# Two gamma loads issued by GpSimd, and the value products of the first two pairs taken in halves of the contraction

## The chip, the cores and the metric

The kernel runs on one core of a Trainium2 chip. The metric is device time in microseconds (us) of one execution; each kernel is executed several times, in rounds with the kernel before on the same chip. Every execution reports two numbers: the time, and the span, which is what the profile covers, from its first to its last instruction. Faster and slower are given at 2%.

PE is the matmul engine, DVE is VectorE, ACT is ScalarE, POOL is GpSimd, SP is SyncE; "SPq" is an instruction of SP's queue that issues a transfer. A turn is a transpose by PE, a cast turns a landed float32 tile into bfloat16. Batch 0's 512 main tokens are worked in two halves of 256; the second is the "second token half". A pair is two times 128 of the 1536 feed-forward columns (blocks 0 and 1 of the weights are the first two pairs), a step is 128 of the 512 rows over which a product sums. The state is the product `kv`.

## The reference, cut to what matters

```python
kv  = einsum('bhsd,bhse->bhde', k, v)                  # batch 8, heads 8, seq 576, head_dim 64
out = einsum('bhsd,bhde->bhse', q, kv)
out = out / sqrt(mean(out*out, -1) + 1e-6) * g_norm
x   = out.transpose(0, 2, 1, 3).reshape(4608, 512)
xn  = x / sqrt(mean(x*x, -1) + 1e-6) * moe_rms_g
g   = xn @ w_gate                                      # 512 x 1536
y   = (g * sigmoid(g) * (xn @ w_val)) @ w_out          # 1536 x 512
```

Both gammas (`g_norm`, `moe_rms_g`) are small vectors. The kernel folds them into the rows of the gate and value weights: those come in as float32, are multiplied by `rowscale` and rounded to bfloat16 once ("rounding" below).

## The kernel before

The order of instructions on each engine is the program's. The program is a long start (batch 0, weights, batch 1, up to about 55 us) and then seven like stages in which PE works without a gap. Only the start is touched. Cuts are marked with `...`.

```python
# loads, in this order; load_kv brings one slice j of k or v
for j in (0, 1):
    load_kv(0, "k", nc.sync, slice(j, j + 1))
    load_kv(0, "v", nc.scalar, slice(j, j + 1))
SC.preload_act_table(ACT.Sqrt)
nc.scalar.dma_start(out=gam[0:NS, :], in_=moe_rms_g...)      # gamma, 2 KB
nc.scalar.dma_start(out=gam[NS : NS + 1, :]..., in_=g_norm...)
load_q0(0, nc.sync)                                          # batch 0's query, first half
for j in (2, 3):
    load_kv(0, "k", nc.sync, slice(j, j + 1))
    load_kv(0, "v", nc.sync, slice(j, j + 1))
load_q0(1, nc.sync)
load_w("g", (0, 1), False)
load_w("v", (0, 1), True)        # value weights of the first two pairs: steps 0,1 then steps 2,3
...
# GpSimd rounds value weights (block, contraction step); ScalarE does step 3
for blk, s in ((0, 0), (0, 1), (1, 0), (0, 2), (1, 1), (1, 2)):
    round_w(blk, "v", s, GP)
...
xs = [Z.scale(c, oZ[c]) for c in range(2)]                   # rows of the second token half
for u in range(2):
    ffn.half_unit(first[1], u, wv_sb, u, 0, 256)             # value products, first pair
for u in range(2):
    x_turn(Z, u, xs[u], DVE)                                 # turns of the second token half
for u in range(2):
    ffn.half_unit(second[1], u, wv_sb, 2 + u, 0, 256)        # value products, second pair
...
load_kv(1, "v", nc.sync)
load_wo(0, (2,))                                             # output weights, block 0, second half
load_q(1)                                                    # batch 1's query
load_wo(1)
...
for c in range(4):
    down_part(c, 0, 2)
att1.kv_products()
...                                                          # casts of batch 1's query
att1.kv_copy()                                               # state out of PSUM: ScalarE and DVE
...
down_part(0, 2, 4)
turns.q_turn(0, SC)                                          # PE turns batch 1's query
down_part(1, 2, 4)
turns.q_turn(1, DVE)
for c in range(2, 4):
    down_part(c, 2, 4)
```

Of the kernel before, what the change touches and what calls it, by code (L numbers as in the profile page):

```python
# [20 lines left out]
def kernel(  # L21
# [12 lines left out]
    nc = tc.nc  # L34
# [10 lines left out]
    NS = d_model // 128  # L45
# [30 lines left out]
    PE, DVE, SC, GP = nc.tensor, nc.vector, nc.scalar, nc.gpsimd  # L76
# [3 lines left out]
    gam = consts.tile([8, 128], FP32, name="gam")  # L80
# [11 lines left out]
    wv_sb = consts.tile([128, NS, d_ff], BF16, name="wv_sb")  # L92
# [91 lines left out]
    def round_w(blk, name, s, engine):  # L184
        j0, j1 = W_BLOCKS[blk]
        dst = {"g": wg_sb, "v": wv_sb}[name][:, s, j0 * 128 : j1 * 128]
        src = w_st[name, blk][:, s, :]
        if engine is SC:
            SC.activation(out=dst, in_=src, func=ACT.Copy, scale=rowscale[:, s : s + 1])
        else:  # L190
            engine.tensor_scalar(  # L191
                out=dst, in0=src, scalar1=rowscale[:, s : s + 1], scalar2=1.0, op0=OP.mult, op1=OP.mult
            )
# [49 lines left out]
    xnts = {}  # L243
# [15 lines left out]
    def to_rows(x, n, c, ps, engine):  # L259

        for j in range(NS):
            PE.matmul(
                ps[:, j, :], lhsT=x[:, 2 * j : 2 * j + 2, :], rhs=identity, is_transpose=True,
                start=(j == 0), stop=(j == NS - 1),
            )
        cast(engine, xnts[n][:, :, 128 * c : 128 * c + 128], ps)
# [198 lines left out]
    class Ffn:  # L465
# [25 lines left out]
        def half_unit(self, ps, u, wt, j, lo, hi):  # L491

            for s in range(NS):
# [2 lines left out]
                    rhs=xnts[self.n][:, s, lo:hi], start=(s == 0), stop=(s == NS - 1),  # L496
                )

        def up_pair(self, i, lo, banks=None):

            banks = banks or self.pair_banks()
            for k, wt in enumerate((wg_sb, wv_sb)):
                for u in range(2):
                    self.half_unit(banks[k], u, wt, 2 * i + u, lo, lo + 256)
            return banks
# [81 lines left out]
    for j in (0, 1):  # L587
        load_kv(0, "k", nc.sync, slice(j, j + 1))
        load_kv(0, "v", nc.scalar, slice(j, j + 1))
    SC.preload_act_table(ACT.Sqrt)  # L590
    nc.scalar.dma_start(out=gam[0:NS, :], in_=moe_rms_g.rearrange("(s p) -> s p", p=128))
    nc.scalar.dma_start(
        out=gam[NS : NS + 1, :].rearrange("o (i d) -> o i d", i=2),
        in_=g_norm.rearrange("(o d) -> o d", o=1).unsqueeze(1).to_broadcast([1, 2, D]),
    )
# [33 lines left out]
    Z = Cols(0, 256, 512, qt0, sqt0, "Z")  # L629
# [44 lines left out]
    def x_turn(cols, c, x, engine, p=att_pool, name="att_ps"):  # L674
        bank = p.tile([128, MAIN], FP32, name=name)
        to_rows(x, cols.n, cols.lo // 128 + c, bank.bitcast(BF16)[:, 0:512].rearrange("p (j t) -> p j t", j=NS), engine)
# [15 lines left out]
    for j in (0, 1):  # L692
# [29 lines left out]
        out=gsq, in0=gcol, scalar=1.0 / d_model, in1=gcol, op0=OP.mult, op1=OP.mult  # L722
# [24 lines left out]
    xs = [A.scale(c, oA[c]) for c in range(2)]  # L747
# [4 lines left out]
        x_turn(A, i, xs[i], DVE, *((ops_pool, "o_ps") if i else ()))  # L752
    round_w(1, "g", 2, DVE)
    round_w(1, "g", 3, SC)
    for blk, s in ((0, 0), (0, 1), (1, 0), (0, 2), (1, 1), (1, 2)):
        round_w(blk, "v", s, GP)
    ffn = Ffn(0)
    first, second = ffn.pair_banks(), ffn.pair_banks()
# [12 lines left out]
        round_w(blk, "v", 3, SC)  # L771
    SC.preload_act_table(ACT.Silu)
    xs = [Z.scale(c, oZ[c]) for c in range(2)]
    for u in range(2):
        ffn.half_unit(first[1], u, wv_sb, u, 0, 256)
    for u in range(2):
        x_turn(Z, u, xs[u], DVE)
    for u in range(2):
        ffn.half_unit(second[1], u, wv_sb, 2 + u, 0, 256)
    ffn.gate_pair(0, 0, first)  # L780
    ffn.gate_pair(1, 0, second)
    for name in ("g", "v"):
# [149 lines left out]
    xs = [F.scale(c, F.outa[c]) for c in range(4)]  # L932
# [50 lines left out]
    for n in range(1, B + 1):  # L983
        ffn = Ffn(n)
# [11 lines left out]
        if n < B:  # L996
# [5 lines left out]
            for i in range(2):  # L1002
                u = o0 + 2 * i
# [63 lines left out]
```

## Time and profile before

| | before |
|---|---|
| time, first three runs | 319.34, 320.76, 320.80 us |
| median of six runs | 320.06 us |
| span of the profiled run | 317.5 us |
| PE busy | 309.2 us, 97% |
| second token half starts (PE) | 21.71 us |
| batch 1's query is cast | 41.74 us |
| first query turn of batch 1 (PE) | 42.63 us, after 0.46 us of idle |

How to read it: PE at 97% says only that PE is rarely idle. What may shorten the time is found by asking, at each idle stretch of PE in the start, which thing came last. The lines for that are in the prediction.

### The profile page before, as it was taken

How to read it: one execution, taken by the hardware profiler on the slowest of the kernel's cores; microseconds unless marked ns; L12 is line 12 of the kernel's file. 1: busy time of each engine (PE TensorE's matmuls, PEld its weight loads, DVE VectorE, ACT ScalarE, POOL GpSimd, SP SyncE). 2: the span in 40 equal slices, each digit the busy share in tenths (PEclk: the TensorE clock that was granted, in tenths of full speed). 3: DMA queues.
4: the chain of work that ended last, by engine and by line, in shares of the span. 5: the costliest groups of instructions: out<-in, count | busy, mean ns of one | idle time of the engine just before them, and what ended most of it. 6: DMA issues, size and time to landing. Idle time of an engine off the chain costs nothing.

```text
span 317.5 us, 6031 instructions
## 1 busy us (share of the span) xinstructions
PE 309.2 (97%) x2371; PEld 149.9 (47%) x2371; DVE 180.5 (57%) x378; ACT 175.7 (55%) x323; POOL 21.4 (7%) x46
## 2 busy tenths in 40 slices
PE   7899999999999999999999999999999999999995
PEld 3585455444444444444444444444444444444443
DVE  3676658579339913892289327941795079504310
ACT  3577457485667465746683768376745374233321
POOL 1274350100000000000000000000000000000000
PEclk9999999999999999999999999999999999999999
DMA  7999999695369167904790489939003610230014
GB/s 277 351 387 387 376 374 343 146 280 196 94 178 369 59 145 194 359 5 113 191 375 19 100 170 231 330 68 200 2 0 61 139 66 3 59 140 3 0 33 100
DMA packets 60712, 54.95 MB, mean 173 GB/s; under 512 B 36232, under 2 KB 45708, under 8 KB 60684
## 3 DMA queue, kind: packets, MB, share of 16 engines
q1 hardware_dynamic: 60304, 53.92, 57.2%
q10 hardware_dynamic: 380, 0.66, 0.6%
q8 instruction: 18, 0.29, 0.4%
q14 instruction: 10, 0.08, 0.1%
HBM read 37.75 MB, written 9.44 MB: 149 GB/s over the span
## 4 chain that ended last, share of the span: by engine, by line
PE 84%; DMA 10%; SPq 3%; ACT 1%; POOL 1%; issue 0%; DVE 0%
PE g_ps L477 27%; PE o_ps L519 26%; PE v_ps L477 26%; DMA st<-in_q_dram 6%; DMA st<-in_moe_w_gate_dram 3%; PE att_ps L286 1%; SPq L199 1%; PE v_ps L519 1%; DMA out_dram<-o_sb 1%; PE att_ps L326 1%; POOL wg_sb L191 1%; SPq L182 1%; SPq L119 1%; PE o_ps L326 0%; PE g_ps L519 0%
## 5 line engine op out<-in xcount | busy, mean ns | idle before, releaser
L483 DVE TENSOR_TENSOR h_sb<-silu,v_ps 128x512 bf16<-128x512 bf16 x104 | 71.1, 684 | 100.4 <-ACT silu L482 68.0
L477 PE MATMUL g_ps<-xnt,wg_sb 128*128 128x512 bf16 x416 | 106.9, 379 | 0.0
L477 PE MATMUL v_ps<-xnt,wv_sb 128*128 128x512 bf16 x416 | 106.8, 379 | 0.0
L482 ACT ACTIVATE silu<-g_ps 128x512 bf16<-128x512 f32 x104 | 62.1, 597 | 70.2 <-PE g_ps L477 58.1
L519 PE MATMUL o_ps<-wo_sb,h_sb 128*128 128x512 bf16 x396 | 87.8, 379 | 0.0
L477 PEld LDWEIGHTS <-wv_sb 128*128 128x128 bf16 x416 | 40.7, 98 | 49.1
L519 PEld LDWEIGHTS <-h_sb 128*128 128x128 bf16 x420 | 40.6, 98 | 47.7 <-issue 0.4
L477 PEld LDWEIGHTS <-wg_sb 128*128 128x128 bf16 x416 | 39.6, 98 | 46.4
L104 ACT COPY o_sb<-o_ps 128x512 f32<-128x512 f32 (+1 forms) x34 | 19.7, 581 | 40.5 <-PE o_ps L519 39.7
L373 DVE TENSOR_TENSOR xna<-outa,s1y 128x512 bf16<-128x512 bf16 x28 | 17.9, 684 | 0.0
L104 ACT CAST vb<-st 128x576 bf16<-128x576 f32 x25 | 15.7, 673 | 3.7 <-DMA st<-in_v_dram 3.7
L356 DVE TENSOR_REDUCE ssq<-sqt 128x16 f32<-128x1024 bf16 x14 | 17.1, 1220 | 0.5
L356 DVE TENSOR_REDUCE ssq<-sq 128x16 f32<-128x1024 bf16 x14 | 17.1, 1220 | 0.5
L104 ACT CAST qb<-st 128x512 bf16<-128x512 f32 (+1 forms) x30 | 16.2, 602 | 2.1 <-DMA st<-in_q_dram 2.0
L104 ACT CAST kb<-st 128x576 bf16<-128x576 f32 x20 | 12.5, 673 | 0.0
L341 ACT ACTIVATE sq<-att_ps 128x512 bf16<-128x512 f32 x14 | 7.6, 594 | 4.3 <-PE att_ps L326 3.6
L355 DVE TENSOR_TENSOR sq<-sq,gsq 128x512 bf16<-128x512 bf16 x14 | 5.9, 422 | 4.9 <-ACT sq L341 4.9
L619 PE MATMUL att_ps<-kv_all 128*128 128x512 bf16 (+1 forms) x23 | 7.5, 445 | 1.2 <-DVE sel L608 1.2
L106 DVE CAST kb<-st 128x576 bf16<-128x576 f32 x12 | 5.7, 498 | 3.8 <-DMA st<-in_k_dram 3.8
L106 POOL CAST wo_sb<-st 128x512 bf16<-128x512 f32 x12 | 7.2, 632 | 7.4 <-DMA st<-in_moe_w_out_dram 7.4
L341 ACT ACTIVATE sqt<-o_ps 128x512 bf16<-128x512 f32 x14 | 7.6, 597 | 0.0
L347 ACT CAST outa<-o_ps 128x512 bf16<-128x512 f32 x14 | 7.5, 591 | 0.0
(145 smaller groups left out, 179.6 us busy)
## 6 DMA issues: line engine op xcount, KB each, us to landing
st<-in_k_dram SPq DMA_DIRECT2D x7, 1152.0 KB, 10.2
st<-in_v_dram SPq DMA_DIRECT2D x7, 1152.0 KB, 12.3
out_dram<-o_sb SPq DMA_DIRECT2D x14, 512.0 KB, 3.1
st<-in_q_dram SPq DMA_DIRECT2D x6, 1024.0 KB, 7.8
st<-in_moe_w_out_dram SPq DMA_DIRECT2D x6, 512.0 KB, 10.4
st<-in_moe_w_gate_dram SPq DMA_DIRECT2D x4, 512.0 KB, 10.1
st<-in_moe_w_val_dram SPq DMA_DIRECT2D x4, 512.0 KB, 9.4
st<-in_k_dram SPq DMA_DIRECT2D x4, 288.0 KB, 4.1
```

The source lines that it names most:

```text
L104: engine.copy(out=dst, in_=src)
L106: engine.tensor_copy(out=dst, in_=src)
L341: SC.activation(out=self.in_place(self.sq[i][:, 0], g), in_=bank, func=ACT.Square)
L347: SC.copy(out=self.in_place(rows, g), in_=bank)
L355: DVE.tensor_tensor(out=sq[:, 1], in0=sq[:, 0], in1=gsq8, op=OP.mult)
L356: DVE.reduce_sum(out=self.ssq[:, c], in_=sq, axis=AX.X)
L373: DVE.tensor_tensor(out=self.xna[c], in0=self.outa[c], in1=self.alpha[:, c, :].to_broadcast([128, H, D]), op=OP.mult)
L477: PE.matmul(ps, lhsT=wt[:, s, j * 128 : (j + 1) * 128], rhs=x[:, s, :], start=(s == 0), stop=(s == NS - 1),)
L482: SC.activation(out=silu, in_=g_ps, func=ACT.Silu)
L483: DVE.tensor_tensor(out=self.h[:, j, :], in0=silu, in1=v_ps, op=OP.mult)
L519: PE.matmul(self.o_ps[c], lhsT=self.h[:, j, c * 128 : (c + 1) * 128], rhs=wo_sb[:, j, :], start=(j == 0), stop=(j == NF - 1),)
L619: PE.matmul(ps[:, 0:w], lhsT=warm_sb[:, 0:128], rhs=warm_sb[:, 0:w], start=True, stop=True, skip_group_check=True)
```

## The change

The intent: two loads fewer on ScalarE's queue, where they take issue time and two of the eight rotating completion semaphores; and PE is to work on the half of the value weights that has landed, on both pairs, and on the turns between, instead of waiting for the other half.

```diff
+        def half_units(self, ps, wt, j, lo, ss):
+            for u in range(2):
+                for s in ss:
+                    PE.matmul(ps[:, u, :], lhsT=wt[:, s, ...], rhs=xnts[self.n][:, s, lo : lo + 256],
+                        start=(u == 0 and s == 0), stop=(u == 1 and s == NS - 1), ...)
...
-    nc.scalar.dma_start(out=gam[0:NS, :], ...)
-    nc.scalar.dma_start(out=gam[NS : NS + 1, :]..., ...)
+    nc.gpsimd.dma_start(out=gam[0:NS, :], ...)
+    nc.gpsimd.dma_start(out=gam[NS : NS + 1, :]..., ...)
...
-    for blk, s in ((0, 0), (0, 1), (1, 0), (0, 2), (1, 1), (1, 2)):
+    for blk, s in ((0, 0), (0, 1), (1, 0), (1, 1), (0, 2), (1, 2)):
         round_w(blk, "v", s, GP)
...
-    for u in range(2):
-        ffn.half_unit(first[1], u, wv_sb, u, 0, 256)
-    for u in range(2):
-        x_turn(Z, u, xs[u], DVE)
-    for u in range(2):
-        ffn.half_unit(second[1], u, wv_sb, 2 + u, 0, 256)
+    ffn.half_units(first[1], wv_sb, 0, 0, (0, 1))
+    ffn.half_units(second[1], wv_sb, 2, 0, (0, 1))
+    x_turn(Z, 0, xs[0], DVE)
+    ffn.half_units(first[1], wv_sb, 0, 0, (2, 3))
+    x_turn(Z, 1, xs[1], DVE)
+    ffn.half_units(second[1], wv_sb, 2, 0, (2, 3))
```

More of the change, by code (lines that the diff above doesn't have):

```diff
@@ L497, in half_unit @@
                 )
+        def half_units(self, ps, wt, j, lo, ss):
+            for u in range(2):
+                for s in ss:
+                    PE.matmul(
+                        ps[:, u, :], lhsT=wt[:, s, (j + u) * 128 : (j + u + 1) * 128],
+                        rhs=xnts[self.n][:, s, lo : lo + 256],
+                        start=(u == 0 and s == 0), stop=(u == 1 and s == NS - 1), skip_group_check=True,
+                    )
         def up_pair(self, i, lo, banks=None):
@@ L590 @@
     SC.preload_act_table(ACT.Sqrt)
-    nc.scalar.dma_start(out=gam[0:NS, :], in_=moe_rms_g.rearrange("(s p) -> s p", p=128))
-    nc.scalar.dma_start(
+    nc.gpsimd.dma_start(out=gam[0:NS, :], in_=moe_rms_g.rearrange("(s p) -> s p", p=128))
+    nc.gpsimd.dma_start(
         out=gam[NS : NS + 1, :].rearrange("o (i d) -> o i d", i=2),
```

## The prediction

> **What bounds the kernel now.** I read the page first, then the chain of waits in order of time, then the instructions in order of time up to 55 us, where the change lies. From the page, parts 1 and 2:
>
> ```profile
> PE 309.2 (97%) x2371; PEld 149.9 (47%) x2371; DVE 180.5 (57%) x378; ACT 175.7 (55%) x323; POOL 21.4 (7%) x46
> ...
> PE   7899999999999999999999999999999999999995
> ...
> DMA  7999999695369167904790489939003610230014
> GB/s 277 351 387 387 376 374 343 146 280 196 94 178 369 59 145 194 359 5 113 191 375 19 100 170 231 330 68 200 2 0 61 139 66 3 59 140 3 0 33 100
> ```
>
> The kernel has two stages. From about 55 us PE is the bound: the chain of waits consists there almost only of PE pieces of 0.86 us. Before that (slices 0 to 6, 7.94 us each), the DMA engines are full: weights, batch 0 and batch 1 all come in at some 380 GB/s. There PE is busy too, so which of the two sets the time has to be read from the chain. The chain over the first 44 us:
>
> ```profile
> 11.15 10.66 DMA st<-in_moe_w_gate_dram
> 21.82 0.08 issue
> 21.90 2.00 POOL wg_sb L191 x4
> 23.90 0.97 SPq L119
> ...
> 28.19 13.53 DMA st<-in_q_dram
> 41.72 0.02 issue
> 41.74 0.41 ACT qb L104
> ...
> 42.63 0.61 PE att_ps L832 x8
> ```
>
> The thing to see is that it holds no PE piece before 42.63. The last link is batch 1's query, issued at 28.19, landing at 41.72. ScalarE casts it and, being in order, only then copies the batch 1 state out of PSUM; that frees the bank which PE's query turn needs. In the timeline of PE:
>
> ```profile
> 40.86 0.78 PE L286 MATMUL att_ps<-vb,kb 64*64 64x64 bf16 x72
> 41.57 0.60 PE L519 MATMUL o_ps<-wo_sb,h_sb 128*128 128x512 bf16 x2
> 42.63 0.61 PE L832 MATMUL att_ps<-identity,qb 128*128 128x128 bf16 x8 [0.46 <-ACT kv_all L104]
> ```
>
> PE runs out of work at 42.17 and idles 0.46 us. So PE has at 42 us a slack of 0.46 us against the transfer. That decides this prediction: whatever PE gains before 42 us becomes idle time there, unless the query also lands earlier.
>
> The query lands when the bytes ahead of it are through. My count: batch 0 (k and v 1.18 MB each, q 1.05), gate and value weights (3.15 each), then k and v of batch 1, half of a first output-weight load twice, and q of batch 1: 14.2 MB. At 385 GB/s, the rate of most stretches, that is 36.8 us; with the first bytes moving about 2 us in, and a dip at 9.5 to 12.5 us (310, 356, 332, 248, 262, 346 GB/s in half-microsecond stretches, worth 0.6 us against 385), it comes to 39.4, near the 41.7 measured. SyncE is not the limit: from 15.7 us its issues take 2.4 to 2.7 us per MB, the pace of a full queue.
>
> **What the Trainium skill says.** "DMA: Bandwidth & Descriptors", section "Issuing engines are not separate DMA queues": transfers started by different engines run on the same 16 DMA engines, so another issuer saves only issue time. The trace agrees as far as it goes: DMA share is 1.0 or more from 3 us on, with two issuers. The same page, "Latency and other measured facts", gives about 1 us to the first byte for a GpSimd issue against 0.6 for SyncE or ScalarE, because software writes the descriptors; this kernel issues none from GpSimd, so no row here shows it. "TensorE: Matmul & The Clock Gate", section "Wait — 56ns, not 53.3ns?": back to back, a warm matmul takes N/2.4 GHz plus 2.5 ns; for 256 columns 0.109 us. The trace agrees: eight of them from 20.83 to the next group at 21.71, 0.11 each (the 273 ns of one is latency). "PSUM — Partial Sum Buffer", section on the matmul accumulator: a first matmul clears the written-bits of its whole 2 KB bank, later ones without the flag overwrite where the bit is clear. So interleaving the contraction of two halves of one bank needs the single start that the change uses; the result should stay right.
>
> **The change, part 1: gamma loads.** It removes two issues from ScalarE (0.55 and 0.71 us, at 1.68 to 2.97). ScalarE was not held by them: its next instruction, a cast at 4.44, waited for the load of v. It puts two issues on GpSimd ahead of the identity matrix, which now is done at 1.3 us and is first needed at 7.9 us; an estimated 1 to 2 us more there is hidden. Gamma is first used at 10.52, so a landing even at 6 us is hidden.
>
> A side effect lies in the instruction order of SyncE. Completion semaphores of the hardware queues rotate over eight, and each issue waits for the landing of the one eight before it, on ScalarE's queue too. Before, the gamma loads took two of the eight. The third k slice waited for the first one's landing (issue at 4.25), the third v slice at 4.63, the fourth ones at 5.68 and 6.05, the second query half at 6.63. Now the third slices wait for nothing (about 3.0 and 3.4), the fourth ones for the first (4.25, 4.63), the query for the second (about 5.7). From the first gate-weight load on, every load waits for the same one as before.
>
> Does an issue 0.6 to 1.4 us earlier land earlier? Only if the queue had run dry. By 4.25 us some 0.79 MB had moved of 1.70 MB issued; by 5.65, 1.37 of 2.29; by 11.5, about 3.4 of 6.5. It never ran dry, so landings should stay within 0.3 us. Gain: 0 to 0.3 us.
>
> **Part 2: value products by halves.** The same 16 matmuls and 8 transposes, same count of weight loads, in another order: contraction steps 0,1 of both pairs, first turn, steps 2,3 of the first pair, second turn, steps 2,3 of the second. GpSimd rounds (1,1) before (0,2). The wait it attacks, in time order before:
>
> ```profile
> 18.91 0.38 PE L494 MATMUL v_ps<-xnt,wv_sb 128*128 128x256 bf16 x2
> 19.13 0.91 ACT L189 ACTIVATE wv_sb<-st,rowscale 128x256 bf16<-128x256 f32 x2 [0.69 <-DMA st<-in_moe_w_val_dram]
> 19.19 1.38 POOL L191 TENSOR_SCALAR wv_sb<-st,rowscale 128x256 bf16<-128x256 f32 x3 [0.70 <-DMA st<-in_moe_w_val_dram]
> 19.72 0.55 PEld L494 LDWEIGHTS <-wv_sb 128*128 128x128 bf16 x6 [0.71 <-POOL wv_sb L191]
> 19.72 0.83 PE L494 MATMUL v_ps<-xnt,wv_sb 128*128 128x256 bf16 x6 [0.43 <-POOL wv_sb L191]
> ```
>
> New order, from 18.80 at 0.109 each: first pair steps 0,1 to 19.24; second pair steps 0,1 to 19.67 (its weights: GpSimd's fourth round, which no longer waits for the later half of the load, at 18.48 + 0.47 = 18.95); turn 0 (scaled rows ready 19.5) to 19.9; first pair steps 2,3 to 20.3 (GpSimd 19.19 + 0.47 = 19.66, ScalarE 19.58); turn 1 (rows ready 20.12, plus some 0.2) to 20.55; second pair steps 2,3 to 20.98 (rounded by 20.13). The copy of turn 1 out of PSUM starts about 20.75, ends 21.16, so the second token half can start at some 21.25. Before: 21.71. PE gains 0.45 us.
>
> Then the margins behind it: block 2 of value is rounded at 25.52 and needed at 26.5 - 0.45; block 4 of gate at 30.95, needed after 31.7. No wait comes in between, so PE reaches 42 us 0.45 us earlier and idles 0.9 us instead of 0.46. Sum on the path: 0 from part 2, 0 to 0.3 from part 1.
>
> **The rivals.** (a) The gain survives: the query lands earlier because earlier issues fill the dip at 9.5 to 12.5. For it: the dip is the one hole in the transfers. Against it: 3 MB were outstanding then, so it is hardly want of issues. It would give up to 0.6 + 0.45 us: 319.1. (b) GpSimd's issues are slow, or their landing is: the gamma transpose at 10.52 delays the rounding factors and all weights behind. Against it: 8 us of room. It would cost 1 to 2 us, of which the query wait hides little of the GpSimd part: 321.5. (c) Earlier loads push others back: k and v get ahead, gate weights later, PE stalls at 16.3. The byte order is unchanged, so I give it little; +0.3 us.
>
> **Range and chances.** The three runs before are 319.34, 320.76 and 320.80, and the profiled one took 319.51: a scatter of 1.4 us, larger than anything worked out above. Their mean is 320.1, and I take 0.1 off: 320.0. The scatter and rivals (a) and (b) give 318.7 to 321.2. Two per cent is 6.4 us, more than the whole of the part touched could give: same 0.98.
>
> **What would show it.** The GpSimd wait inside the value products gone, the second token half starting near 21.25, and the idle time of PE before the first query turn grown to about 0.9 us, with the query landing at 41.4 to 41.8: then the steps hold. The query landing before 41.2 would show rival (a) and refute my byte count; a PE wait at the gamma transpose or at the first turn of queries would show (b). From 55 us on, the PE pieces should be the same; a difference there would be outside this reasoning.

## The result, and the profile after

The changed kernel took 319.80 us (median of 6, 319.60 to 320.17), the kernel before 320.06 (median of 6). The ratio is 0.9992, 95% interval 0.9973 to 1.0011. Ratios here are the mean time of one kernel's runs over that of the other's of the same rounds, so not quite the ratio of the medians quoted. Executions over 1.5% slower than the fastest of the same kernel are left out of the means. Predicted were 320.0 us and "same" at 0.98.

So the number was right. The traces show that two of the steps behind it were not. First the value products in the changed kernel, in order of time (start, duration, engine, line, operation, out<-in, then the idle time before it and what ended it):

```profile
18.25 2.74 POOL L191 TENSOR_SCALAR wv_sb<-st,rowscale 128x256 bf16<-128x256 f32 x6 [1.33 <-DMA st<-in_moe_w_val_dram]
...
19.01 0.95 PE L503 MATMUL v_ps<-xnt,wv_sb 128*128 128x256 bf16 x5
...
20.14 0.50 PE L503 MATMUL v_ps<-xnt,wv_sb 128*128 128x256 bf16 x3 [0.17 <-POOL wv_sb L191]
...
21.36 0.60 PE L503 MATMUL v_ps<-xnt,wv_sb 128*128 128x256 bf16 x4
21.56 0.42 DVE L106 COPY xnt<-att_ps 128x512 bf16<-128x512 bf16 x1 [0.23 <-PE att_ps L262]
...
22.04 1.03 PE L494 MATMUL o_ps<-xnt,wg_sb 128*128 128x256 bf16 x8
```

GpSimd now makes its six roundings in one go from 18.25, not three from 17.07 and three from 19.19. It waited 1.33 us for the *first* half of the value weights, which before had landed while it was still busy with gate weights. PE follows those roundings, and the second token half (last line) starts at 22.04: later than the 21.71 of before, not earlier, and nowhere near the predicted 21.25.

Then the chain of waits about the batch 1 query, changed kernel (start, duration, what):

```profile
28.76 13.43 DMA st<-in_q_dram
42.19 0.02 issue
42.21 0.40 ACT qb L104
...
43.10 0.61 PE att_ps L842 x8
```

and PE there:

```profile
41.19 0.78 PE L286 MATMUL att_ps<-vb,kb 64*64 64x64 bf16 x72
41.90 0.61 PE L529 MATMUL o_ps<-wo_sb,h_sb 128*128 128x512 bf16 x2
43.10 0.61 PE L842 MATMUL att_ps<-identity,qb 128*128 128x128 bf16 x8 [0.59 <-ACT kv_all L104]
```

The chain has the same links as before, 0.47 us later: cast at 42.21 against 41.74, PE's turn at 43.10 against 42.63. The span is 317.9 against 317.5. Taking one from the other, span minus cast is 275.7 in the changed kernel and 275.8 before. In these two profiles everything after the query's landing is rigid.

The hole in the transfers at 9.5 to 12.5 us is gone: 373 GB/s there against 309 before. But the first 8 us moved less (262 against 278), and up to 17 us both moved 5.4 MB. The filled hole brought no earlier query, which was rival (a). In part the hole was chance: a second profile of the kernel before has 341 GB/s there.

### The profile page after: what moved, and what is told of

Read it like the earlier page. It is cut to its first block, busy times and chain, and to the rows that moved or that the text cites. A ratio compares the mean times of both kernels' runs of the same rounds, so it can differ in the third digit from the quotient of the medians.

```text
span 317.9 us, 5995 instructions
## 1 busy us (share of the span) xinstructions
PE 308.1 (97%) x2334; PEld 149.9 (47%) x2371; DVE 180.9 (57%) x378; ACT 175.6 (55%) x323; POOL 22.6 (7%) x48
## 4 chain that ended last, share of the span: by engine, by line
PE 82%; DMA 10%; SPq 3%; ACT 1%; issue 1%; another core or an unknown queue 1%; POOL 1%; DVE 0%
PE v_ps L477 26%; PE g_ps L477 26%; PE o_ps L529 25%; DMA st<-in_q_dram 4%; DMA st<-in_moe_w_gate_dram 3%; DMA st<-in_v_dram 2%; PE att_ps L286 1%; SPq L199 1%; SPq L119 1%; PE v_ps L529 1%; DMA out_dram<-o_sb 1%; PE att_ps L326 1%; POOL wg_sb L191 1%; SPq L182 1%
## 5 line engine op out<-in xcount | busy, mean ns | idle before, releaser
L477 PE MATMUL g_ps<-xnt,wg_sb 128*128 128x512 bf16 x398 | 104.7, 379 | 0.7
L529 PE MATMUL o_ps<-wo_sb,h_sb 128*128 128x512 bf16 x386 | 86.8, 379 | 0.4
L104 ACT COPY o_sb<-o_ps 128x512 f32<-128x512 f32 (+1 forms) x34 | 19.7, 579 | 40.5 <-PE o_ps L529 36.9
L104 ACT CAST kb<-st 128x576 bf16<-128x576 f32 x20 | 12.5, 673 | 0.0
L347 ACT CAST outa<-att_ps 128x512 bf16<-128x512 f32 x14 | 7.5, 592 | 0.0
```

The costliest lines, as they stand in the source:

```text
L104: engine.copy(out=dst, in_=src)
L347: SC.copy(out=self.in_place(rows, g), in_=bank)
L477: PE.matmul(ps, lhsT=wt[:, s, j * 128 : (j + 1) * 128], rhs=x[:, s, :], start=(s == 0), stop=(s == NS - 1),)
L529: PE.matmul(self.o_ps[c], lhsT=self.h[:, j, c * 128 : (c + 1) * 128], rhs=wo_sb[:, j, :], start=(j == 0), stop=(j == NF - 1),)
```

## The experiments

Twelve runs were made. The first four were to tell whether the later landings came from the change or from chance. The next four test each suspected gain or cost by itself, the last four a version in which the query does not hold PE. Mean spans are over all runs of a kernel in its job; the kernel before had mean spans of 317.98, 318.00 and 317.95 in the three jobs (11 runs each, 317.3 to 319.0).

| run | ratio to before (95%) | mean span, us | lowest to highest | time minus span |
|---|---|---|---|---|
| changed kernel, its own six runs | 0.9992 (0.9973 to 1.0011) | 317.53 | 317.3 to 317.9 | 2.31 |
| b_again | 0.9998 (0.9979 to 1.0016) | 317.93 | 317.6 to 318.5 | 2.01 |
| a_again | 1.0002 (0.9988 to 1.0016) | 317.78 | 317.6 to 318.1 | 2.29 |
| gam_only | 0.9998 (0.9983 to 1.0013) | 317.63 | 317.4 to 318.0 | 2.31 |
| halves_only | 1.0001 (0.9983 to 1.0019) | 318.07 | 317.5 to 318.7 | 2.02 |
| sw_dummy | 1.0017 (0.9998 to 1.0035) | 318.27 | 317.6 to 319.0 | 2.30 |
| gam_first | 1.0059 (1.0032 to 1.0085) | 319.87 | 318.6 to 321.2 | 2.05 |
| less_pe | 1.0046 (1.0015 to 1.0076) | 319.48 | 318.2 to 320.8 | 2.02 |
| q_first | 0.9995 (0.9979 to 1.0011) | 317.68 | 317.0 to 318.4 | 2.05 |
| q_first_again | 0.9978 (0.9959 to 0.9997) | 317.53 | 316.8 to 318.7 | 2.05 |
| q_first_halves | 0.9981 (0.9962 to 1.0001) | 317.40 | 316.8 to 318.2 | 2.05 |
| q_first_share | 0.9968 (0.9950 to 0.9986) | 317.10 | 316.6 to 317.6 | 1.93 |
| q_first_share_gam | 0.9973 (0.9956 to 0.9989) | 317.02 | 316.8 to 317.5 | 2.16 |

All results were correct except less_pe. Its output is wrong, which doesn't matter for the time.

### b_again and a_again: both kernels once more

No edit.

> The kernel before, unchanged, once more. Theory (the span is set by the landing of batch 1's query, and everything after is rigid): span minus landing of that query is again 275.8 us, within 0.15, whatever the landing. Rival 1 (the later landings in the changed kernel, 18.15 against 17.0 us for the first half of the value weights and 42.19 against 41.72 for the query, come from the moved gamma loads): this profile shows 17.0 and 41.7 again, within 0.2. Rival 2 (they are scatter from run to run): they differ from the first profile by up to 1 us. Ratio to before 1.000 within 0.002 in all theories.

> The changed kernel, once more. Theory: span minus query landing 275.7 within 0.15. Rival 1 (gamma loads cause the later landings): first half of the value weights again near 18.1, query near 42.2, second token half starts near 22.0. Rival 2 (scatter): those move by up to 1 us, and if the value weights land by 17.1 the second token half starts at 21.25 as predicted. Ratio to before 0.998 to 1.001.

The kernel before, second profile: the value rounding and the query turn, in order of time:

```profile
18.41 2.75 POOL L191 TENSOR_SCALAR wv_sb<-st,rowscale 128x256 bf16<-128x256 f32 x6 [0.99 <-DMA st<-in_moe_w_val_dram]
...
20.30 0.83 PE L494 MATMUL v_ps<-xnt,wv_sb 128*128 128x256 bf16 x6 [0.62 <-POOL wv_sb L191]
...
22.29 0.93 PE L494 MATMUL o_ps<-xnt,wg_sb 128*128 128x256 bf16 x7
...
43.66 0.61 PE L832 MATMUL att_ps<-identity,qb 128*128 128x128 bf16 x8 [0.90 <-ACT kv_all L104]
```

The same kernel, but its first half of the value weights now lands at 18.3 instead of 17.0, its second token half starts at 22.29 instead of 21.71, and its query is cast at 42.77 instead of 41.74. Rival 2, scatter, holds: the first profile, on which the prediction was built, was a lucky one. In all 13 other profiles GpSimd starts the value roundings at 17.7 to 19.3. Span minus cast is again 275.7 (318.5 - 42.77), as the theory asks, though the landing moved by a whole microsecond. The changed kernel's second profile is like its first: GpSimd from 18.33, second half from 22.12, cast at 42.18, span 317.8.

### gam_only and halves_only: each part alone

```diff
 gam_only: before.py with
-    nc.scalar.dma_start(out=gam...)      # both
+    nc.gpsimd.dma_start(out=gam...)      # both
 halves_only: after.py with
-    nc.gpsimd.dma_start(out=gam...)      # both
+    nc.scalar.dma_start(out=gam...)      # both
```

> Gamma loads from GpSimd alone, value products as before. Rival 1: value weights' first half lands near 18.1, the query near 42.2, no hole in the transfers at 11 to 12 us; PE starts the second token half at 22.1 or later; ratio 1.000 to 1.002. Rival 2: landings spread about those of before, ratio 0.999 to 1.001. Theory: span is query landing + 275.7 within 0.15.

> Value products by halves alone, gamma loads on ScalarE as before. Theory: value weights land near 17.0, second token half starts at 21.25 (before 21.71), PE reaches the batch 1 query turn about 0.45 us earlier and idles there about 0.9 us instead of 0.46, the query lands at 41.7 within 0.3, ratio 0.999 to 1.001. Rival 3 (PE is the bound after all): ratio 0.9986 (0.45 us less). Rival 2: value weights land at random between 17.0 and 18.2, and the start of the second half follows them.

gam_only, then halves_only, each in order of time:

```profile
18.41 2.75 POOL L191 TENSOR_SCALAR wv_sb<-st,rowscale 128x256 bf16<-128x256 f32 x6 [1.46 <-DMA st<-in_moe_w_val_dram]
...
22.30 0.93 PE L494 MATMUL o_ps<-xnt,wg_sb 128*128 128x256 bf16 x7
```

```profile
18.36 2.75 POOL L191 TENSOR_SCALAR wv_sb<-st,rowscale 128x256 bf16<-128x256 f32 x6 [0.95 <-DMA st<-in_moe_w_val_dram]
...
22.15 1.03 PE L494 MATMUL o_ps<-xnt,wg_sb 128*128 128x256 bf16 x8
```

To compare them whatever the landing, count from GpSimd's first value rounding to the start of the second token half. Without the halves: 22.30 - 18.41 = 3.89, and 3.88 in b_again. With them: 22.15 - 18.36 = 3.79, and 3.79 in both profiles of the changed kernel. The halves give PE 0.1 us, every time; predicted were 0.45. The reason is that in both orders PE waits for GpSimd's *fourth* rounding: step 2 of the first pair before, step 1 of the second pair after the change. Six roundings in a row last 2.75 us, so the fourth is done some 1.84 us after the first begins. PE's wait ends there: 0.62 us at 20.30 in b_again, 0.17 us at 20.14 in the changed kernel. What follows takes 1.99 us in the old order (20.30 to 22.29) and 1.90 in the new one (20.14 to 22.04). There the last link is DVE's copy of the second turn, which ends at 21.98. The sixth rounding holds nobody: in the changed kernel it ends at 20.99, and the products that need it start at 21.36.

That 0.1 us does not reach the end either. The halves_only span was 318.3 with the query cast at 42.50; PE had idled 0.77 us before its turn. Ratio 1.0001, so rival 3 (PE is the bound) is not supported. Its size would have been below what the ratio can tell, so the argument rests on span minus cast: 275.8 here, 275.6 in gam_only and a_again, 275.7 in the changed kernel and b_again, 275.8 before, while PE's idle time before the turn went from 0.39 (gam_only) to 0.90 (b_again).

The rival that the gamma loads cause later landings is refuted. gam_only's landings look like it, but without these loads (b_again, halves_only) the value weights and the query land as late. Of halves_only's own theory nothing but the ratio came true: the weights landed at about 18.3 instead of 17.0, and the start and the query followed. Instead the six gam_only runs have a *shorter* mean span, 317.63, than the kernel before. Over all 18 runs with the change's gamma loads (changed kernel 317.53, a_again 317.78, gam_only 317.63, six each) the mean is 317.65 and the highest 318.1, against 317.98 and 319.0 in 33 runs of the kernel before. Yet the times are equal. The last column of the table says why: with loads from GpSimd the time is the span plus 2.3 us, without them plus 2.0. (The last two rows, with 1.93 and 2.16, lie 0.1 lower; why is not known, but the difference between them is nearly the same.)

### sw_dummy: the price of a load from GpSimd, by itself

```diff
     nc.scalar.dma_start(out=gam...)      # both stay
+    nc.gpsimd.dma_start(out=spare...)    # the same two loads, into an unused tile
```

> The kernel before, plus the same two small loads issued once more by GpSimd into an unused tile; gamma itself stays on ScalarE. In the five profiles so far, the time of a run is its span plus 2.0 us without a GpSimd load (all runs of b_again and halves_only) and plus 2.3 us with it (all runs of a_again and gam_only). Theory A (a load from GpSimd costs 0.3 us outside the span): time minus span 2.3, span like before (mean 318.0, scatter 317.4 to 318.9), so the mean time is 0.3 us longer: ratio 1.001. Rival B (the 0.3 us comes with the freed slots of the semaphore rotation): time minus span 2.0, ratio 1.000.

Theory A holds: time minus span was 2.24 to 2.34 in the six runs, and 1.99 to 2.08 in the 11 runs of the kernel before beside them. Two small loads from GpSimd add about 0.26 us that no profile shows, since it lies outside the span; whether ahead of it or behind it the runs do not tell. Rival B falls.

In this run the semaphores rotate as before (two slots go to gamma), and the spans scatter from 317.6 to 319.0 as before. The shorter, narrower spans thus go with taking the gamma loads off ScalarE and not with GpSimd issuing something. Whether the freed slots do it or ScalarE's saved issue time, no run tells apart.

### gam_first: free the semaphores without GpSimd

```diff
+    nc.scalar.dma_start(out=gam...)      # both, moved ahead of the first k and v loads
     for j in (0, 1):
         load_kv(0, "k", nc.sync, slice(j, j + 1))
         load_kv(0, "v", nc.scalar, slice(j, j + 1))
```

> Gamma loads stay on ScalarE but are its first two issues, ahead of the first two v slices; their semaphores are then free when the third k and v slices reuse them, so those are issued at about 3.1 us as in the changed kernel, and nothing is issued by GpSimd. Theory A: time minus span 2.0. Theory C (the freed rotation is what narrows and shortens the span, mean 317.65 over 18 runs with gamma on GpSimd against 318.0 over 21 runs without): spans 317.3 to 318.1, mean 317.7, ratio 0.999. Rival D (it is the issuer that does it, or chance): spans scatter to 318.5 and over, mean 318.0, ratio 1.000.

This failed: 0.6% slower. The third k slice was issued at 3.10 us as expected, but the run was meant to test theory C and cannot, for another cost came in. The profile is of the slowest of the six runs. In order of time, then PE and the rest in stretches (from:to, length, busy us and instructions of PE, PEld, DVE, ACT, POOL, then granted clock of PE, DMA share, GB/s):

```profile
7.65 0.67 ACT L104 CAST vb<-st 128x576 bf16<-128x576 f32 x1 [3.21 <-DMA st<-in_v_dram]
8.37 0.69 PE L254 MATMUL att_ps<-vb,kb 64*64 64x64 bf16 x18 [3.45 <-ACT vb L104]
```

```profile
6.00:8.00 2.00, 0.00 (x0) 0.00 (x0) 0.00 (x0) 0.35 (x1) 0.00 (x0) 0.95 1.04 390
8.00:10.00 2.00, 1.63 (x21) 0.83 (x20) 0.72 (x2) 1.53 (x3) 0.00 (x0) 0.50 1.05 400
```

The first v slice was issued at 2.05 instead of 0.72 us and landed at 7.6 instead of 4.4: the 1.3 us of later issue cost 3.2 us. The trace has the bytes of each DMA queue: from 2.0 to 3.5 us SP's queue moved 0.46 MB and ScalarE's next to nothing; from 4.0 to 7.5 us they moved 0.51 and 0.56 MB. So the late start of ScalarE's bytes cost the time, and then its two v slices went through side by side. Why they start so late is not shown. PE idled 3.45 us, its granted clock fell to 0.50, and it stayed there until past 14 us. Here an early issue of the first v slices was worth more than anything the semaphores gave.

### less_pe: take PE work away ahead of the query

```diff
+            ns = 2 if self.n == 0 and j in (7, 9) else NS
-                for s in range(NS):
+                for s in range(ns):
```

> The kernel before with 8 matmuls fewer (half of the contraction of two feed-forward blocks of the first batch, at about 31 and 35 us; the result is wrong on purpose), that is 1.73 us less work for PE ahead of the batch 1 query. Theory (the query's landing sets the end): PE idles 2.2 to 2.6 us before the first batch 1 query turn instead of 0.46 to 0.9, span minus landing stays 275.7, ratio 1.000 within 0.002. Rival (PE is the bound there): span 1.7 us shorter, ratio 0.9946.

Neither came true. PE did idle longer, but the span grew. Order of time, and stretches as above:

```profile
43.31 0.61 PE L833 MATMUL att_ps<-identity,qb 128*128 128x128 bf16 x8 [2.06 <-ACT kv_all L104]
```

```profile
43.00:44.00 1.00, 0.63 (x9) 0.57 (x10) 0.54 (x3) 0.30 (x2) 0.18 (x1) 1.00 1.09 395
44.00:45.00 1.00, 1.00 (x10) 0.69 (x10) 0.10 (x1) 0.97 (x1) 0.99 (x2) 0.80 0.98 364
45.00:46.00 1.00, 1.00 (x4) 0.30 (x2) 0.59 (x1) 0.00 (x0) 0.85 (x2) 0.50 1.07 368
```

The query was cast at 42.42, so 1.73 us of PE work less did not bring PE's turn forward: that part of the theory stands. But the idle stretch of 2.06 us was followed, about 1 us after PE had taken up work again, by some 3.5 us at a granted clock of about 0.50, and span minus cast came to 277.9 instead of 275.7. Two of the four runs had spans of 320.3 and 320.8, the other two 318.2 and 318.6. The theory lacked this: PE time saved ahead of a wait is worth nothing, and where the clock falls after it, less than nothing. Only one run was profiled; the mean granted clock was 0.995 in three of the four (spans 320.3, 320.8 and 318.6) and 0.999 in the fourth. The rival, 1.7 us shorter, is excluded.

### q_first and q_first_again: the query ahead, so that PE no longer waits for it

```diff
     load_kv(1, "v", nc.sync)
-    load_wo(0, (2,))
     load_q(1)
+    load_wo(0, (2,))
...
-            ps = att_pool.tile([128, NS, 2, 128], BF16, name="att_ps")       # in q_turn
+            p, nm = ((gps_pool, "g_ps"), (vps_pool, "v_ps"))[pair]
+            ps = p.tile([128, NS, 2, 128], BF16, name=nm)
...
-    down_part(0, 2, 4)
     turns.q_turn(0, SC)
-    down_part(1, 2, 4)
     turns.q_turn(1, DVE)
-    for c in range(2, 4):
-        down_part(c, 2, 4)
+    for j in (2, 3):
+        for c in range(4):
+            down_part(c, j, j + 1)
```

> The kernel before with batch 1's query loaded ahead of the second half of the first output-weight block (0.52 MB, 1.36 us at 385 GB/s), its turns put into the banks of the up products so that they do not wait for the copy of the state, and the down products of steps 2 and 3 put behind both turns. Theory (the query landing holds the kernel, PE alone is 0.46 to 0.9 us shorter): query lands at 40.4 to 41.4, PE does not idle at the turns, span 0.3 to 0.8 us shorter, ratio 0.9978 to 0.999. Rival 1 (PE is the bound anyway): ratio 1.000. Rival 2 (the wait moves to the output weights, landing at about 42.2 and cast by GpSimd until 43.4): PE idles there by up to 0.6 us, ratio 1.000.

> q_first once more, to stand beside the next three on one chip. Its profile had no idle of PE at the query turns and a chain of PE pieces from 21 us on; its span of 317.0 was the start of the second token half, 21.68, plus 295.3. Theory: span minus that start is 295.3 within 0.2 again; mean span 317.6 to 317.8; ratio 0.9985 to 0.9995. Rival (the query still holds it in most runs): span minus start varies by more than 0.4.

q_first, in order of time:

```profile
17.80 2.75 POOL L191 TENSOR_SCALAR wv_sb<-st,rowscale 128x256 bf16<-128x256 f32 x6 [0.53 <-DMA st<-in_moe_w_val_dram]
...
21.68 1.04 PE L494 MATMUL o_ps<-xnt,wg_sb 128*128 128x256 bf16 x8
...
40.84 0.78 PE L286 MATMUL att_ps<-vb,kb 64*64 64x64 bf16 x72
41.55 0.62 PE L833 MATMUL g_ps<-identity,qb 128*128 128x128 bf16 x8
42.00 0.61 PE L833 MATMUL v_ps<-identity,qb 128*128 128x128 bf16 x8
```

The turns carry no idle mark any more: the query's last cast starts at 40.56 and PE goes straight from the state products into them. The chain of waits is now one of PE pieces from 19.7 us, behind GpSimd's value roundings and behind the landing of the value weights. The bound has moved from the query to those weights: in q_first_again they came late (GpSimd from 19.34), the second token half started at 23.23, and the span was 318.7. Span minus that start: 295.3 in q_first, 295.5 in q_first_again. So rival 2 of q_first (waiting for the output weights) did not come about, nor did the one of q_first_again.

The gain in the span is as small as the theory said, but too small for one job to prove: mean spans 317.68 and 317.53 against 318.00 and 317.95, ratios 0.9995 and 0.9978, the second with an interval that excludes 1. Both ratios lie outside what was expected (0.9978 to 0.999 and 0.9985 to 0.9995), and q_first's alone does not tell the theory from rival 1; the moved chain does. The three parts of the edit were not tried apart.

### q_first_halves, q_first_share, q_first_share_gam: the change on top

q_first_halves is q_first with the change's value products and rounding order, gamma on ScalarE. q_first_share gives one of GpSimd's roundings to ScalarE:

```diff
-    for blk, s in ((0, 0), (0, 1), (1, 0), (1, 1), (0, 2), (1, 2)):
+    for blk, s in ((0, 0), (0, 1), (1, 1), (0, 2), (1, 2)):
         round_w(blk, "v", s, GP)
...
     Z.root_by_table(lambda: None)
+    round_w(1, "v", 0, SC)
```

q_first_share_gam is that with gamma from GpSimd.

> q_first plus the value products by halves (gamma on ScalarE). Theory (the 0.2 us that the halves give PE with the weights landing at 18.3 was absorbed by the query wait, which is gone here): second token half starts about 3.7 us after the value weights' first half lands (3.9 to 4.0 without the halves), span minus start 295.3 as in q_first, mean span 0.2 us below q_first_again. Rival (the halves are worth nothing on the path): mean span equal to q_first_again within 0.1, span minus start larger by 0.2.

> q_first_halves with one of GpSimd's six value roundings (0.46 us) given to ScalarE, which is idle then. Theory (with the weights landing at 18.3 instead of 17.0 the chain of six GpSimd roundings sets the pace of the value products): second token half starts 3.2 to 3.4 us after the landing, 0.3 to 0.5 us earlier than in q_first_halves, mean span 0.3 to 0.5 us below it; ratio to before 0.9970 to 0.9985. Rival (ScalarE's rounding or the landing of the later half holds it): start no earlier, span equal.

> q_first_share with gamma loaded by GpSimd as in the changed kernel. Theory: time minus span 2.3 instead of 2.0 (0.3 us outside the span), spans in a narrower band (0.8 us or less from lowest to highest, against 1.4 without), mean span at most 0.3 us shorter than q_first_share; so mean time equal to it or up to 0.3 us longer. Rival (the freed rotation lands the weights later, near 18.3 always): mean span 0 to 0.3 us longer, time 0.3 to 0.6 us longer.

q_first_share, in order of time:

```profile
17.74 2.30 POOL L191 TENSOR_SCALAR wv_sb<-st,rowscale 128x256 bf16<-128x256 f32 x5 [0.52 <-DMA st<-in_moe_w_val_dram]
...
21.09 1.03 PE L494 MATMUL o_ps<-xnt,wg_sb 128*128 128x256 bf16 x8
...
42.26 0.59 PE L529 MATMUL o_ps<-wo_sb,h_sb 128*128 128x512 bf16 x2 [0.24 <-POOL wo_sb L106]
```

From GpSimd's first rounding to the second token half: 3.88 in q_first, 3.89 in q_first_again, 3.80 in q_first_halves, 3.35 in q_first_share and in q_first_share_gam. One rounding fewer in GpSimd's row, 0.46 us, gives 0.45 us. This shows what held the halves back: (1,1), the rounding that PE waited for, is now GpSimd's third. Span minus start stays 295.3 to 295.5 in all five, so here the gain reaches the end: the mean span falls from 317.53 (q_first_again) to 317.40 and 317.10. The first of these steps, 0.13, is below the scatter; by the traces it should be 0.09, not the 0.2 expected.

The last line shows the next bound: in q_first_share (and in q_first_share_gam, by 0.23 us) PE waits for output weights that land at 41.54 and that GpSimd then casts. That is rival 2 of q_first, come about one step later. PE time gained in the start beyond this would be lost there again.

Gamma from GpSimd on top: mean span 317.02, a narrower band (0.7 us against 1.0), but 0.2 us more outside the span, so 319.17 us mean time against 319.03. Outside the span 2.3 us in all were expected and 2.16 found. It gives back what it gains, if the 0.08 us in the span are a gain at all: they are below the scatter.

q_first_share is the fastest version found: 0.9968 of the kernel before (0.9950 to 0.9986), that is 1 us, of which 0.85 is in the span and 0.11 outside it, unexplained. The changed kernel has 0.9992 and 1.0002.

## Why the prediction was right, and where its steps were wrong

That 320.0 lay so near 319.80 is luck within a scatter of 1.4 us; "same" at 2% was safe, since no gain or loss that was worked out came near 6.4 us. What can be judged is the mechanism.

**The frame held.** That batch 1's query decides the end, and that PE time gained before it is lost there, is shown by span minus cast, 275.6 to 275.8 in six profiles of before, after and the two halves of the change, with landings a microsecond apart (sw_dummy: 276.0). less_pe confirms for 1.73 us of work that PE's turn does not come earlier, with the clock as a cost that the prediction did not have.

**The term of the value products was mis-sized: 0.1 us, not 0.45.** The step that failed is "GpSimd's fourth round, which no longer waits for the later half of the load, at 18.48 + 0.47". It took the landing of the first half of the value weights from a single profile. That profile had it at 17.0; in all others GpSimd starts at 17.7 or later. With the later landing GpSimd ends its fourth rounding at 20.08 in the changed kernel, not at 18.95, and PE waits for it as it did before; the new order only leaves 0.1 us less to do after it. Predicted start of the second token half 21.25, found 22.04 and 22.12. Whether the halves would give 0.45 us with a landing at 17.0 no run shows, for no other profile starts so early.

**The idle time before the query turn** was predicted at 0.9 us and was 0.59 and 0.48, for the same reason; the query's landing also scatters (42.2, not the 41.4 to 41.8 named as a sign), so one profile of each would not have told.

**The gamma term** was put at 0 to 0.3 us. In the span it was 0.33 (mean of 18 runs against 33), but about 0.26 came back outside the span, which the prediction did not count, because no view of a profile shows it. Sum: some 0.07 us less, plus nothing from the halves, against a measured 0.0008 of 320, or 0.26, in the first job and +0.06 us in a_again's. All within the scatter.

**The argument about early issues was half right.** By bytes issued and moved the queue never ran dry. The third k slice, issued at 3.11, landed at 8.7; in the two profiles of the kernel before it was issued at 4.25 and 4.58 and landed at 8.1 and 8.7. Here issues that came earlier did not land earlier. Why the spans are nevertheless shorter and less scattered with gamma off ScalarE is open: sw_dummy speaks against GpSimd's issuing, gam_first was spoilt, and no run shows the mechanism.

**Three readings in it were loose.** The byte count came to 39.4 us, and "near the 41.7 measured" hides 2.3 us, five times the gain in question: by 41.72 us the queue had moved 14.9 MB (357 GB/s on average), 0.7 more than was counted. The DMA share is not 1.0 or more all the way from 3 us on; it is 0.89 from 11 to 12 us. And SyncE's issues do not go by size: 1.18 MB of v took 1.17 us to issue, 0.52 MB of output weights 2.69.

**Of the rivals,** (a) fell: the hole was filled, without effect on the query. (b) fell as put: GpSimd's gamma loads took 0.69 and 0.52 us to issue and some 4.5 to 4.9 us to land, still by about 6.5, ahead of the use at 10.63. It pointed at the right engine, though; the cost lay outside the profile. (c) did not come about here; gam_first, where v came 1.3 us later behind SP's loads and landed 3.2 us later, shows what such a push can cost.

## What to carry to other kernels

Before working a gain out of one profile, look whether the landing times it rests on repeat: here the landings of the kernel before moved by 1.0 to 1.3 us between two profiles, more than any term of the sum. Measure each step from the event that starts it (the landing) and the end from the event that sets it; such differences repeated to 0.2 us where the times scatter by 1.5. And when a change shortens the span and not the time, subtract the one from the other in every run.

## What the Trainium skill lacked or had wrong

- "DMA: Bandwidth & Descriptors", "Issuing engines are not separate DMA queues", says that another issuing engine saves only issue time. It has no word of a cost outside the profile: two small loads from GpSimd put the time minus the span at 2.24 to 2.34 us, against 1.99 to 2.08 without (sw_dummy and the kernel before beside it).
- The same page, "Latency and other measured facts", gives about 1 us to the first byte for a GpSimd load. In the changed kernel, by the trace's record of DMA packets, GpSimd's queue moved no packet from 1.2 to 5.0 us, though its loads were issued at 1.26 and 1.94; its first packet ran at 5.08. From issue to landing 2 KB took 4.85 us and 0.5 KB 4.50.
- The same page, "Queues, rings and completion order", has each transfer engine take turns between the queues. gam_first agrees once both queues run: 0.56 MB of ScalarE's queue beside 0.51 MB of SP's from 4.0 to 7.5 us. What the page lacks is when a load's turn begins: the first v slice, issued at 2.05, had its first bytes only near 3.8 us. Why is open.
- "TensorE: Matmul & The Clock Gate", Part 1, has the clock fall after an idle window of about 3.4 us. In less_pe the one gap was 2.06 us. The granted clock fell about 1 us after its end, after a stretch with the query turns and a single other product, and was 0.50 from 45 to 48 us. So a gap shorter than the window can be followed by a fall; whether the turns counted as idle the run does not tell.
- No page has the rotation of completion semaphores seen in this kernel's instruction order, by which a load waits for the landing of the one eight before it, whether SP or ScalarE issued that: the third k slice went out at 4.25, when the first had landed at 4.2, and at 3.11 once gamma no longer took two of the eight.
